# Attention over columns and a soft mixture of experts on one core: batches that share a tile of q and k, one set of 22 buffers, other split pairs and a new order

## The chip, the cores and the metric

The kernel runs on one core of a Trainium2 chip. The metric is the device time of one execution in microseconds, from the start of the program to its end. The engines are PE (TensorE, with its weight loads listed as PEld), DVE (VectorE), ACT (ScalarE), POOL (GpSimd) and SP (SyncE), which issues all DMA transfers of this kernel on one queue.

## The reference

Inputs are q, k and v of shape 4 x 5056 x 256, a scalar tau, phi (256 x 32) and the weights of eight experts, w1 (256 x 1024 each) and w2 (1024 x 256 each), all float32.

```python
qn = q / (norm(q, axis=1) + 1e-6)          # per batch and column, over the 5056 rows
kn = k / (norm(k, axis=1) + 1e-6)
a  = softmax(kn.T @ qn / tau)              # 256 x 256 per batch
x  = (v @ a).reshape(4 * 5056, 256)

logits = x @ phi                           # 20224 x 32
d  = softmax(logits, axis=0)               # over all rows
slot_input = d.T @ x                       # 32 slots, 4 per expert
slot_out[e] = relu(slot_input[e] @ w1[e]) @ w2[e]
out = softmax(logits, axis=1) @ slot_out   # 20224 x 256
```

## The kernel before

**Tiles.** A batch's 5056 rows are padded to 5120, ten units of four tiles of 128 rows; with four batches there are NU = 40 units, numbered u. `load_qk` (L127) brings q and k of one unit as 1 MB, 8 KB in each of 128 partitions, into a `raw` tile. v comes in twenty blocks p of eight tiles (`load_v`, L135, 1 MB). Each block's transpose `vt`, in two halves m of 512 KB (480 KB for a batch's last block), is needed for the logits: a half is either loaded (`load_vt`, L141 and L143, for the pairs in the set `LT`) or made on PE by four `turn` transposes (L355) per half block h, which ACT copies out of PSUM (`turned`, L360).

**Scores.** `score(u, j)` (L230) adds k.T @ q of one tile to a batch's sum in PSUM. In a raw tile it is one float32 matmul for each half of the columns. In a split tile, ACT casts q and k to a rounded high part (`cast`, L186), DVE subtracts to get the low part (`low`, L192), and three matmuls high x high, high x low, low x high take its place. The table `NS` splits the first two tiles of every unit but the first, 39 pairs. For the column norms ACT squares a unit (`square`, L207, tile `sq`) and DVE adds it to the batch's first `sq` tile (`add`, L213); `att_sums` folds that (L236).

**After a batch's scores** a chain of short `att_` steps makes the softmax `a` and M = a @ phi. `logits` (L383) multiplies the transposed v with M, and `gather` (L483) sums v under the row weights into slots. The last batch's slots go through the experts: `up` (L667), `flip_h`, `down` (L701) in two halves of the output columns, with w1 (`load_w1`, L651, eight loads of 1 MB) and w2 (`load_w2`, L656, sixteen loads of 512 KB, one per expert and half). `out_mul` (L741) and `out_evict` (L763 on ACT, L765 on DVE) make 1 MB output tiles, or halves of them for batch 0, and `store` (L771, L773) writes them.

**Buffers.** There are five `raw` tiles, three `sq`, three `hl` (high and low parts), six `v`, two `pre` tiles for early w2 loads, all 8 KB in a partition, and six `vt` tiles of 4 KB. `HOME` says which `raw` tile a unit takes; the others go round. A tile is used again once its last readers are done.

**Order.** Every step is put in a list by `at` or `tail`, and `ORDER`, a written permutation of that list, is the order in which they are issued. Each engine, and SP with its transfers, runs its own steps in that order. So a transfer whose buffer is not free yet holds back all transfers behind it.

Of the kernel before, what the change touches and what calls it, by code (L numbers as in the profile page):

```python
# [85 lines left out]
def colnorm_attention_soft_moe(  # L86
# [96 lines left out]
    def cast(u):  # L183
        ns = NS[u]
        hl = apool.tile([P, 2, 4, C], F32R, tag="hl", name=f"hl{u}", bufs=3)
        act.copy(hl[:, :ns, 0::2, :], raws[u][:, :ns])  # L186
        hls[u] = hl

    def low(u):
        ns = NS[u]  # L190
        hl = hls[u]
# [896 lines left out]
```

## Time and profile before

| What | Value |
|---|---|
| median of 3 runs | 280.6 us (280.35 to 280.88) |
| profiled execution | 279.4 us |
| its span, first to last instruction | 277.6 us |
| PE, DVE, ACT, POOL busy | 252.0, 233.1, 190.7, 7.4 us |
| moved by DMA | 112.98 MB, mean 407 GB/s |

The span is what the trace covers; the time of an execution has about 1.8 us more around it. The busy time of PE is made from matmuls whose ends are modelled, so short gaps between them do not show. A row of a timeline begins with the start and the length in us, and ends with the idle time of its engine before it and what ended that idle time.

### The profile page before, as it was taken

What the parts mean: (1) busy time and instruction counts of PE and PEld (TensorE: products, weight loads), DVE (VectorE), ACT (ScalarE), POOL (GpSimd) and SP (SyncE); (2) the same over time, 40 slices, a digit from 0 to 9 for tenths busy, and PEclk for the clock granted to TensorE, in tenths of its full rate; (3) what the DMA queues carried; (4) which work ended last, traced back from release to release, by engine and by line L of the source; (5) the groups of instructions that cost most, each with busy time, mean ns of one, the idle gap of its engine ahead of it and who ended that gap; (6) DMA issues with size and microseconds to landing.
All of it is one profiled execution on the core that took longest, in us unless ns stands there. A gap on an engine that the chain in (4) does not pass through costs nothing. (4 is left out here: it accounts for less than half of the span.)

```text
span 277.6 us, 6058 instructions
## 1 busy us (share of the span) xinstructions
PE 252.0 (91%) x2462; PEld 208.6 (75%) x2462; DVE 233.1 (84%) x343; ACT 190.7 (69%) x275; POOL 7.4 (3%) x10
## 2 busy tenths in 40 slices
PE   7998999999999999999999999999999999776600
PEld 7897999999898996999788878766544778466400
DVE  1598999999999999988998987559999879997620
ACT  4986898999898698897688943697417248544420
POOL 1000000200001100020000001000000000000000
PEclk9999999999999999999999999999999999955955
DMA  7999999999999999999999999999999999999996
GB/s 276 427 417 420 420 413 424 420 417 417 417 417 421 411 422 421 415 419 414 421 411 415 412 426 411 413 420 419 418 410 409 387 364 392 414 418 417 414 423 254
DMA packets 19179, 112.98 MB, mean 407 GB/s; under 512 B 2256, under 2 KB 2256, under 8 KB 8528
## 3 DMA queue, kind: packets, MB, share of 16 engines
q1 hardware_dynamic: 19152, 112.60, 98.9%
q8 instruction: 19, 0.31, 0.5%
q14 instruction: 8, 0.07, 0.1%
HBM read 91.62 MB, written 20.97 MB: 406 GB/s over the span
## 5 line engine op out<-in xcount | busy, mean ns | idle before, releaser
L213 DVE TENSOR_TENSOR sq<-sq,sq 128x1024 f32<-128x1024 f32 (+1 forms) x63 | 85.0, 1370 | 3.1 <-ACT sq L207 2.6
L207 ACT ACTIVATE sq<-raw 128x2048 f32<-128x2048 f32 x40 | 76.4, 1914 | 12.0 <-DMA raw<-in_qk_dram 5.9
L230 PE MATMUL S<-raw 128*128 128x256 f32 x328 | 76.8, 380 | 1.3 <-DMA raw<-in_qk_dram 1.3
L230 PE MATMUL S<-hl 128*128 128x256 f32 x468 | 68.3, 295 | 0.0
L230 PEld LDWEIGHTS S<-raw 128*128 128x128 f32 x328 | 59.8, 190 | 9.4 <-DMA raw<-in_qk_dram 2.2
L230 PEld LDWEIGHTS S<-hl 128*128 128x128 f32 x468 | 60.4, 190 | 1.3
L192 DVE TENSOR_TENSOR hl<-raw,hl 128x1024 fp32r<-128x1024 f32 x39 | 47.0, 1220 | 9.5 <-ACT hl L186 9.5
L186 ACT CAST hl<-raw 128x1024 fp32r<-128x1024 f32 x39 | 40.4, 1045 | 8.1 <-PE S L230 4.1
L741 PE MATMUL op_None<-so,lg 32*128 32x256 f32 x240 | 23.4, 481 | 6.0 <-DVE lg L631 4.1
L741 PEld LDWEIGHTS op_None<-so,lg 32*128 32x128 f32 x240 | 18.5, 231 | 10.3 <-ACT o L763 7.7
L763 ACT COPY o<-op_None 128x512 f32<-128x512 f32 x30 | 15.7, 594 | 15.2 <-PE op_None L741 7.8
L765 DVE COPY o<-op_None 128x512 f32<-128x512 f32 x30 | 19.0, 676 | 4.7 <-PE op_None L741 4.7
L355 PE MATMUL vTp<-ident,v 128*128 128x128 f32 x136 | 20.2, 277 | 0.0
L483 PE MATMUL G<-v,dn 128*32 128x256 f32 x320 | 19.5, 381 | 0.0
L355 PEld LDWEIGHTS vTp<-ident,v 128*128 128x128 f32 x136 | 15.7, 145 | 3.3 <-issue 1.2
L383 PE MATMUL L<-vt,M 128*32 128x256 f32 (+1 forms) x272 | 17.0, 379 | 0.0
L360 ACT COPY vt<-vTp 128x512 f32<-128x512 f32 x26 | 15.0, 582 | 2.6 <-PE vTp L355 2.6
L483 PEld LDWEIGHTS G<-v,dn 128*32 128x32 f32 x320 | 9.7, 110 | 7.1 <-issue 0.8
L383 PEld LDWEIGHTS L<-vt,M 128*32 128x32 f32 x272 | 8.5, 110 | 5.5 <-ACT x L360 0.3
L741 PE MATMUL op<-so,lg 32*128 32x128 f32 x160 | 8.9, 311 | 2.9 <-DVE o L765 1.7
L763 ACT COPY o<-op 128x256 f32<-128x256 f32 x20 | 6.4, 377 | 6.7 <-PE op L741 6.7
L252 POOL TENSOR_TENSOR rn<-rn,half 128x4 f32<-128x4 f32 x4 | 6.7, 1662 | 163.4 <-DVE rn L247 163.4
(111 smaller groups left out, 238.9 us busy)
## 6 DMA issues: line engine op xcount, KB each, us to landing
raw<-in_qk_dram SPq DMA_DIRECT2D x40, 1024.0 KB, 10.0
v<-in_v_dram SPq DMA_DIRECT2D x20, 1024.0 KB, 12.2
out_dram<-o SPq DMA_DIRECT2D x15, 1024.0 KB, 8.6
vt<-in_vt_dram SPq DMA_DIRECT2D x17, 512.0 KB, 11.0
w<-in_moe_w_dram SPq DMA_DIRECT2D x16, 512.0 KB, 11.0
w<-in_moe_w_dram SPq DMA_DIRECT2D x8, 1024.0 KB, 15.0
out_dram<-o SPq DMA_DIRECT2D x10, 512.0 KB, 4.7
vt<-in_vt_dram SPq DMA_DIRECT2D x4, 480.0 KB, 8.8
```

Source lines behind the costliest of these rows:

```text
L186: act.copy(hl[:, :ns, 0::2, :], raws[u][:, :ns])
L192: dve.tensor_tensor(hl[:, :ns, 1::2, :], raws[u][:, :ns], hl[:, :ns, 0::2, :].bitcast(F32), op=ALU.subtract)
L207: act.activation(sq, raws[u], AF.Square)
L213: dve.tensor_tensor(a[:, lo:hi], a[:, lo:hi], s[:, lo:hi], op=ALU.add)
L230: pe.matmul(sm, w, x, start=first, stop=False, skip_group_check=True)
L355: pe.transpose(tp[:, P * jj : P * jj + P], vs[p][:, 4 * h + jj, P * m : P * m + P], ident)
L360: act.copy(x[:, h * UT : h * UT + UT], tps[p, h, m])
L383: pe.matmul(L[S * g : S * g + S, :n, :], M[:, m, :], x[:, :n, S * g : S * g + S], start=m == 0, stop=m == 1,)
L483: pe.matmul(gp[S * g : S * g + S, :C], dn[:, x, j, :], vt[:, j, :], start=x == 0 and j < G, stop=x == n - 1 and j >= G,)
L741: pe.matmul(ops[b, p, hf, g][:, h, :], cT[b][S * g : S * g + S, 4 * i : 4 * i + 4, :].rearrange("s j t -> s (j t)"), so[S * g : S * g + S] ...
L763: act.copy(dst, src)
L765: dve.tensor_copy(dst, src)
```

## The change

- **Shared tiles.** Batches 0 and 1, and batches 2 and 3, are packed together: the last tile of unit 9 (and 29) holds the last 64 rows of one batch and the first 64 of the next (`MIX`). Unit 10 (and 30) then has three tiles. `score` does the mixed tile in two halves of 64 partitions, one for each batch's sum; `square_next` puts the second half's squares into the next batch's `sq` tile after a memset on POOL; `add` takes the rest in two pieces.
- **Split pairs.** `SPLIT` names 43 pairs of tiles (u, k), two tiles each, in place of `NS`. `cast` and `low` work on one pair, and each pair has a tile of its own.
- **Buffers.** All tiles of 8 KB are one set of 22, and `HOME` gives each its place: `raw`, `sq`, `hl`, `v`, the transposed v as `x` with both halves, `nat`, w1, w2, `hs`, `hT` and outputs.
- **w2** is laid out in blocks of 1 MB, two experts and one half of the columns each: eight loads.
- **vt.** (10, 0) and (14, 0) leave `LT` and are made by `turn` and `turned`, which now use two PSUM banks, T0 and X1, in place of T0 for most.
- The first load is issued as one tile and three tiles. `ORDER` is new.

The diff, with `HOME` and `ORDER` cut to the parts that are spoken of:

```diff
-NS = [0] + [2] * (NU - 1)
-LT = {(p, 0) for p in (0, 2, 3, 4, 5, 6, 7, 8, 9, 10, 11, 12, 13, 14, 15, 18, 19)} | {(p, 1) for p in (0, 3, 6, 9, 12, 15)}
+MIX = (UB - 1, 3 * UB - 1)
+SPLIT = {(u, 0) for u in range(1, NU) if u not in (1, 2, 3, 17, 20, 27, 31)} | {(u, 1) for u in (2, 5, 14, 24, 26, 27, 31, 33, 35, 37, 39)}
+LT = {(p, 0) for p in (0, 2, 3, 4, 5, 6, 7, 8, 9, 11, 12, 13, 15, 18, 19)} | {(p, 1) for p in (0, 3, 6, 9, 12, 15)}
...
+    "raw31": 11, "sq28": 9, "sq29": 6, "sq30": 14, "hl29_0": 18, "hl26_0": 5, "hl27_1": 16, "sq26": 10, "x7": 6,
+    "sq27": 21, "raw30": 15, "v3": 9, "v8": 21, "raw32": 3, "hl26_1": 15, "hl31_1": 18, "sq31": 1, "hl32_0": 20,
+    "sq32": 5, "hl30_0": 2, "x6": 10, "v11": 15, "raw33": 12, "raw34": 0, "raw37": 1, "raw38": 17, "hl33_1": 2,
+    "sq33": 15, "hl34_0": 10, "hl33_0": 8, "x8": 11, "sq37": 2, "sq34": 16, "hl37_1": 9, "raw39": 4, "v6": 12,
+    "v10": 7, "x9": 9, "x12": 1, "x11": 13, "raw36": 5, "raw35": 3, "hl38_0": 6, "sq39": 20, "hl37_0": 18, "sq38":
...
-    vpool = ctx.enter_context(tc.tile_pool(name="vpool", bufs=6, reuse_waits="tile"))
-    tpool = ctx.enter_context(tc.tile_pool(name="tpool", bufs=1, reuse_waits="tile"))
...
+    def big(name, shape, dt=F32):
+        return apool.tile(shape, dt, tag=f"big{HOME[name]}", name=name)
+
+    def tiles(u):
+        return 3 if u - 1 in MIX else 4
+
+    def load_qk(u, parts=None):
         b, i = divmod(u, UB)
-        raw = apool.tile([P, 4, 2, C], F32, name=f"raw{u}", **raw_home(f"raw{u}"))
-        for lo, hi in parts:
+        raw = big(f"raw{u}", [P, 4, 2, C])
+        for lo, hi in parts or ((0, tiles(u)),):
...
-    load_qk(0)
+    load_qk(0, ((0, 1), (1, 4)))
...
+    def cast(u, k):
+        hl = big(f"hl{u}_{k}", [P, 2, 4, C], F32R)
+        act.copy(hl[:, :, 0::2, :], raws[u][:, 2 * k : 2 * k + 2])
+        hls[u, k] = hl
...
     def square(u):
+        n = tiles(u)
+        act.activation(sq_tile(u)[:, :n], raws[u][:, :n], AF.Square)
+
+    def square_next(u):
+        sq = sq_tile(u + 1)
+        pool.memset(sq[:HD, 3], 0.0)
+        act.activation(sq[HD:, 3], raws[u][HD:, 3], AF.Square)
 
     def add(u, lo, hi):
         b, i = divmod(u, UB)
         a, s = sqs[b * UB], sqs[u]
-        dve.tensor_tensor(a[:, lo:hi], a[:, lo:hi], s[:, lo:hi], op=ALU.add)
+        if u in MIX and hi == 4:
+            if lo < 3:
+                dve.tensor_tensor(a[:, lo:3], a[:, lo:3], s[:, lo:3], op=ALU.add)
+            dve.tensor_tensor(a[:HD, 3], a[:HD, 3], s[:HD, 3], op=ALU.add)
+        else:
+            dve.tensor_tensor(a[:, lo:hi], a[:, lo:hi], s[:, lo:hi], op=ALU.add)
+
+    def score(u, j, split):
+        b = u // UB
+        mixed = u in MIX and j == 3
+        rows = ((b, 0, HD), (b + 1, HD, P)) if mixed else ((b, 0, P),)
...
-    def load_w2(e, h, tag):
-        if e not in w2t:
-            w2t[e] = slot(tag, f"w2_{e}").rearrange("p (x q) c -> p x (q c)", x=2)
-        sp.dma_start(w2t[e][:, h], w2[e, h][:, : NF * P])
+    def load_w2(k, h):
+        w2t[k, h] = big(f"w2_{k}_{h}", [P, 8, C]).rearrange("p (x q) c -> p x (q c)", x=2)
+        sp.dma_start(w2t[k, h], w2[k, h][:, : 2 * NF * P].rearrange("p (x f) -> p x f", x=2))
...
-                at(t, turn, p, h, m, T0)
+                at(t, turn, p, h, m, (T0, X1)[h])
...
-    x[:, :N, 0], x[:, :N, 1] = q, k
+    both = np.stack([q, k], axis=2)
+    x[0::2, :N] = both[0::2]
+    x[0::2, N:] = both[1::2, : P // 2]
+    n3 = 3 * P
+    x[1::2, :n3] = both[1::2, P // 2 : P // 2 + n3]
+    x[1::2, UT:] = both[1::2, P // 2 + n3 :]
```

## Rows read from the trace of the kernel before

**Rows 1.** The page: span, busy engines, GB/s by slice, the DMA queue, bytes.
```profile
span 277.6 us, 6058 instructions
...
PE 252.0 (91%) x2462; PEld 208.6 (75%) x2462; DVE 233.1 (84%) x343; ACT 190.7 (69%) x275; POOL 7.4 (3%) x10
...
GB/s 276 427 417 420 420 413 424 420 417 417 417 417 421 411 422 421 415 419 414 421 411 415 412 426 411 413 420 419 418 410 409 387 364 392 414 418 417 414 423 254
...
q1 hardware_dynamic: 19152, 112.60, 98.9%
...
HBM read 91.62 MB, written 20.97 MB: 406 GB/s over the span
```

**Rows 2.** Table by stage: stage, length, busy of PE/PEld/DVE/ACT/POOL, clock, DMA share, GB/s.
```profile
9.20:126.00 116.80, 115.91 (x832) 104.81 (x831) 111.77 (x115) 103.28 (x103) 5.64 (x3) 1.00 1.02 419
...
126.00:177.00 51.00, 51.00 (x503) 42.85 (x502) 43.68 (x76) 35.85 (x59) 1.01 (x1) 1.00 1.02 416
177.00:204.80 27.80, 27.13 (x362) 17.73 (x362) 22.94 (x65) 16.91 (x48) 0.00 (x0) 1.00 1.02 418
204.80:220.30 15.50, 15.09 (x228) 8.15 (x227) 14.94 (x18) 6.60 (x10) 0.00 (x0) 1.00 1.02 408
220.00:230.00 10.00, 9.53 (x249) 7.56 (x242) 8.11 (x18) 4.42 (x15) 0.00 (x0) 1.00 0.91 358
```

**Rows 3.** Waits of the SP queue: total us, times, longest us.
```profile
SPq L127 <- DVE hl L192: 58.8, 22, 4.4
```

**Rows 4.** Timeline of PE's weight loads that were held by a transfer.
```profile
165.80 0.59 PEld L483 LDWEIGHTS G<-v,dn 128*32 128x32 f32 x16 [0.36 <-DMA v<-in_v_dram]
...
205.73 0.16 PEld L667 LDWEIGHTS H<-w,slT 128*32 128x32 f32 x8 [0.83 <-DMA w<-in_moe_w_dram]
```

**Rows 5.** Timeline around the end of the reads: stores issued, the second half's `down`.
```profile
221.90 10.86 SPq L773 DMA_DIRECT2D out_dram<-o  x9
...
224.68 2.02 PE L701 MATMUL O<-w,hT 128*32 128x128 f32 x64
```

**Rows 6.** The page's DMA issues, w2: count, KB each, us to landing.
```profile
w<-in_moe_w_dram SPq DMA_DIRECT2D x16, 512.0 KB, 11.0
```

**Rows 7.** Timeline of the start: first loads issued, first and second landed.
```profile
0.74 2.56 SPq L127 DMA_DIRECT2D raw<-in_qk_dram  x5
...
5.61 1.91 ACT L207 ACTIVATE sq<-raw 128x2048 f32<-128x2048 f32 x1 [3.39 <-DMA raw<-in_qk_dram]
...
8.10 1.05 ACT L186 CAST hl<-raw 128x1024 fp32r<-128x1024 f32 x1 [0.57 <-DMA raw<-in_qk_dram]
```

**Rows 8.** PE: timeline of scores one behind another, and the group of transposes.
```profile
68.79 2.75 PE L230 MATMUL S<-raw 128*128 128x256 f32 x12
71.19 2.49 PE L230 MATMUL S<-hl 128*128 128x256 f32 x18
73.61 1.72 PE L383 MATMUL L<-vt,M 128*32 128x256 f32 x28
...
L355 PE MATMUL vTp<-ident,v 128*128 128x128 f32 x136 | 20.2, 277 | 0.0
```

**Rows 9.** Timeline of DVE: `low` and half adds one behind another.
```profile
65.51 1.22 DVE L192 TENSOR_TENSOR hl<-raw,hl 128x1024 fp32r<-128x1024 f32 x1
66.64 2.35 DVE L213 TENSOR_TENSOR sq<-sq,sq 128x1024 f32<-128x1024 f32 x2
68.91 1.22 DVE L192 TENSOR_TENSOR hl<-raw,hl 128x1024 fp32r<-128x1024 f32 x1
```

**Rows 10.** Groups by line and shape: count, busy us, mean ns, idle before.
```profile
L360 ACT COPY vt<-vTp 128x512 f32<-128x512 f32 x26 | 15.0, 582 | 2.6 <-PE vTp L355 2.6
...
L236 DVE TENSOR_TENSOR sq<-sq 128x512 f32<-128x512 f32 x4 | 2.7, 680 | 0.1
```

**Rows 11.** Timeline of the last `low` on DVE and the last scores on PE.
```profile
170.42 1.22 DVE L192 TENSOR_TENSOR hl<-raw,hl 128x1024 fp32r<-128x1024 f32 x1
...
175.32 1.68 PE L230 MATMUL S<-hl 128*128 128x256 f32 x12
```

More of the change, by code (lines that the diff above doesn't have):

```diff
@@ L133, in load_v @@
         b, i = divmod(p, PB)
-        vs[p] = slot("v" if p < 17 else "raw", f"v{p}")
+        vs[p] = big(f"v{p}", [P, 8, C])
         sp.dma_start(vs[p], v8[b, i][:, : 8 * C].rearrange("p (j c) -> p j c", c=C))
@@ L181, in colnorm_attention_soft_moe, with low, sq_tile @@
     hls = {}
[L183 to L191, printed above, removed]
+    def cast(u, k):
+        hl = big(f"hl{u}_{k}", [P, 2, 4, C], F32R)
+        act.copy(hl[:, :, 0::2, :], raws[u][:, 2 * k : 2 * k + 2])
+        hls[u, k] = hl
+    def low(u, k):
+        hl = hls[u, k]
         dve.tensor_tensor(
-            hl[:, :ns, 1::2, :], raws[u][:, :ns], hl[:, :ns, 0::2, :].bitcast(F32), op=ALU.subtract
+            hl[:, :, 1::2, :], raws[u][:, 2 * k : 2 * k + 2], hl[:, :, 0::2, :].bitcast(F32), op=ALU.subtract
         )
-    sqtag = {}
-    free = [0, 1, 2]
-    for b in range(B):
-        sqtag[b * UB] = free[0]
-        o = free[1:]
-        for i in range(1, UB):
-            sqtag[b * UB + i] = o[(i - 1) % 2]
-        free = [o[1], o[0], free[0]]
-    def square(u):
-        sq = apool.tile([P, 4, 2, C], F32, tag=f"sq{sqtag[u]}", name=f"sq{u}")
-        act.activation(sq, raws[u], AF.Square)
-        sqs[u] = sq
+    def sq_tile(u):
+        if u not in sqs:
+            sqs[u] = big(f"sq{u}", [P, 4, 2, C])
+        return sqs[u]
+    def square(u):
+        n = tiles(u)
[4 more added lines that the diff above has]
+        act.activation(sq[HD:, 3], raws[u][HD:, 3], AF.Square)
     def add(u, lo, hi):
@@ L212, in add @@
         a, s = sqs[b * UB], sqs[u]
-        dve.tensor_tensor(a[:, lo:hi], a[:, lo:hi], s[:, lo:hi], op=ALU.add)
-    def score(u, j):
-        b, i = divmod(u, UB)
-        first = "S" not in st[b]
-        if first:
-            st[b]["S"] = bank((S0, S1)[b % 2], f"S{b}")
+        if u in MIX and hi == 4:
[8 more added lines that the diff above has]
+        rows = ((b, 0, HD), (b + 1, HD, P)) if mixed else ((b, 0, P),)
+        first = {x[0]: "S" not in st[x[0]] for x in rows}
         for m in range(2):
-            sm = st[b]["S"][:, C * m : C * m + C]
             cols = slice(P * m, P * m + P)
-            if j >= NS[u]:
-                raw = raws[u]
-                ops_ = [(raw[:, j, 1, cols], raw[:, j, 0, :])]
-            else:
-                hl = hls[u]
-                ops_ = [(hl[:, j, x, cols], hl[:, j, y, :]) for x, y in ((2, 0), (2, 1), (3, 0))]
-            for w, x in ops_:
-                pe.matmul(sm, w, x, start=first, stop=False, skip_group_check=True)
-                first = False
+            for bb, lo, hi in rows:
+                if first[bb] and m == 0:
+                    st[bb]["S"] = bank((S0, S1)[bb % 2], f"S{bb}")
+                sm = st[bb]["S"][:, C * m : C * m + C]
+                if split:
+                    hl = hls[u, j // 2][:, j % 2]
+                    ops_ = [(hl[:, x, cols], hl[:, y, :]) for x, y in ((2, 0), (2, 1), (3, 0))]
+                else:
+                    raw = raws[u][lo:hi, j]
+                    ops_ = [(raw[:, 1, cols], raw[:, 0, :])]
+                for w, x in ops_:
+                    pe.matmul(sm, w, x, start=first[bb], stop=False, skip_group_check=True)
+                    first[bb] = False
     def att_sums(b, lo):
@@ L337, in att_m @@
         st[b]["M"] = M
-    tps, xs = {}, {}
+    tps = {}
+    xs = {}
     def vt_tile(p, m):
-        if (p, m) not in vts:
-            if p < 17:
-                vts[p, m] = tpool.tile([P, 8 * P], F32, tag=f"vt{m}", name=f"vt{p}_{m}", bufs=3)
-            else:
-                if p not in xs:
-                    xs[p] = apool.tile([P, 2, 8 * P], F32, tag=f"sq{XT[p]}", name=f"x{p}")
-                vts[p, m] = xs[p][:, m]
+        if p not in xs:
+            xs[p] = big(f"x{p}", [P, 2, 8 * P])
+        vts[p, m] = xs[p][:, m]
         return vts[p, m]
@@ L415, in logit_nat @@
         if b not in nat:
[L416 removed]
+            t = big(f"nat{b}", [P, 8, C]).rearrange("p j c -> p (j c)")
             nat[b] = t[:, : 8 * PB * S].rearrange("p (j s) -> p j s", s=S)
@@ L637, in colnorm_attention_soft_moe, with load_w1 @@
     w1t, w2t = {}, {}
-    def slot(tag, name):
-        if tag == "v":
-            return vpool.tile([P, 8, C], F32, tag="v", name=name)
-        if tag == "raw":
-            return apool.tile([P, 8, C], F32, name=name, **raw_home(name))
-        if tag == "hl":
-            return apool.tile([P, 8, C], F32, tag=tag, name=name, bufs=3)
-        return apool.tile([P, 8, C], F32, tag=tag, name=name, bufs=2 if tag == "pre" else None)
-    def load_w1(e, tag):
-        t = slot(tag, f"w1_{e}")
+    def load_w1(e):
+        t = big(f"w1_{e}", [P, 8, C])
         w1t[e] = t.rearrange("p (d x) c -> p d (x c)", d=2)
         sp.dma_start(w1t[e], w1[e][:, : 2 * F].rearrange("p (d f) -> p d f", d=2))
-    def load_w2(e, h, tag):
-        if e not in w2t:
-            w2t[e] = slot(tag, f"w2_{e}").rearrange("p (x q) c -> p x (q c)", x=2)
-        sp.dma_start(w2t[e][:, h], w2[e, h][:, : NF * P])
+    def load_w2(k, h):
+        w2t[k, h] = big(f"w2_{k}_{h}", [P, 8, C]).rearrange("p (x q) c -> p x (q c)", x=2)
+        sp.dma_start(w2t[k, h], w2[k, h][:, : 2 * NF * P].rearrange("p (x f) -> p x f", x=2))
     hss, hps, hTs, htp = {}, {}, {}, {}
@@ L662, in up @@
         if r not in hss:
-            hss[r] = tpool.tile([P, F], F32, tag="vt1", name=f"hs{r}", bufs=3)
+            hss[r] = big(f"hs{r}", [P, F])
         hp = bank(hb[r, x], f"H{r}_{x}")
@@ L687, in back_h @@
         if r not in hTs:
-            hTs[r] = tpool.tile([P, NF, P], F32, tag="vt0", name=f"hT{r}", bufs=3)
+            hTs[r] = big(f"hT{r}", [P, NF, P])
         (act.copy if x else dve.tensor_copy)(hTs[r][:, 4 * x : 4 * x + 4, :], htp[r, x])
@@ L703, in down @@
                     hTs[r][:, f, S * g : S * g + S],
-                    w2t[G * r + g][:, h, P * f : P * f + P],
+                    w2t[2 * r + g // 2, h][:, g % 2, P * f : P * f + P],
                     start=first and f == f0,
@@ L723, in o_back @@
         act.copy(sos[0][:, h], fo[h][:, :P])
-    OT = ["raw"] * 3 + ["hl"] * 3 + ["v"] * 6 + ["raw"] * 5 + ["hl"] * 3
     rings = {0: [S0, S1, LB, GB, T0, X0], 1: [S0, S1, LB, GB, T0, X0, T1, X1]}
@@ L752, in out_evict @@
         if (b, p) not in ots:
-            ots[b, p] = slot(OT[b * PB + p], f"o{b}_{p}")
+            ots[b, p] = big(f"o{b}_{p}", [P, 8, C])
         ot = ots[b, p]
@@ L791, in colnorm_attention_soft_moe @@
         first = i == 0
-        ns = NS[u]
-        if ns:
-            at(u - 1.08, cast, u)
-            at(u - (0.62 if first else 0.95), low, u)
+        for k in range(2):
+            if (u, k) in SPLIT:
+                at(u - 1.08, cast, u, k)
+                at(u - (0.62 if first else 0.95), low, u, k)
+                for j in (2 * k, 2 * k + 1):
+                    at(u + (0.45 if odd else 0.05) + 0.15 * j, score, u, j, 1)
         at(u - 0.65, square, u)
-        grp = [p for p in range(14) if 2 * p + FV == u and group(p)[2] == group(p)[3] - 1]
+        if u in MIX:
+            at(u - 0.64, square_next, u)
         if i:
@@ L803, in colnorm_attention_soft_moe @@
                 at(u + 0.60, add, u, 0, 4)
-        for j in range(ns):
-            at(u + (0.45 if odd else 0.05) + 0.15 * j, score, u, j)
         raw_at = u if first and u else u - (0.30 if u % 2 or u < FV else 0.04) if u else -0.6
-        for j in range(ns, 4):
-            at(raw_at + 0.001 * j, score, u, j)
+        for j in range(tiles(u)):
+            if (u, j // 2) not in SPLIT:
+                at(raw_at + 0.001 * j, score, u, j, 0)
         if u + NRAW < NU:
@@ L908, in colnorm_attention_soft_moe @@
                 t = 2.0 + 0.5 * (4 * (p - 15) + 2 * h + m)
-                tail(t, turn, p, h, m, (T0, T1)[h] if p > 15 else T0)
+                tail(t, turn, p, h, m, (T0, X1)[h])
                 tail(t + 0.05, turned, p, h, m)
@@ L977, in colnorm_attention_soft_moe @@
     tail(23.6, last_back)
-    for t, e, tag in (
-        (0.6, 0, "raw"), (0.6, 1, "raw"), (0.6, 2, "hl"), (0.61, 3, "hl"), (0.61, 4, "hl"),
-        (7.2, 5, "v"), (10.1, 6, "v"), (11.1, 7, "v"),
-    ):
-        tail(t, load_w1, e, tag)
-    for t, e, tag in (
-        (17.3, 0, "v"), (17.31, 1, "v"), (17.32, 2, "v"),
-        (19.2, 5, f"sq{XT[19]}"), (22.3, 6, "raw"), (22.4, 7, "raw"),
-    ):
+    for e in range(8):
+        tail(0.6 + e, load_w1, e)
+    for k in range(4):
         for h in range(2):
-            tail(t + 4 * h, load_w2, e, h, tag)
-    for e in (3, 4):
-        for h in range(2):
-            tail(20 + h, load_w2, e, h, "pre")
+            tail(17.3 + 4 * h, load_w2, k, h)
     for b, ts_ in ((0, (10.4, 10.5, 10.6, 13.8, 17.0, 17.1, 17.2)), (1, (18.9, 19.0, 19.1, 20.0, 20.5, 20.6, 20.7)),
@@ L1077 @@
     add("moe_w1", apart(w1.reshape(len(w1), P, -1)))
-    add("moe_w2", apart(w2.reshape(len(w2), P, -1, 2, P).transpose(0, 3, 1, 2, 4).reshape(len(w2), 2, P, -1)))
+    x = w2.reshape(len(w2) // 2, 2, P, -1, 2, P).transpose(0, 4, 2, 1, 3, 5)
+    add("moe_w2", apart(x.reshape(len(w2) // 2, 2, P, -1)))
     out_ap = nc.dram_tensor("out_0_dram", (B, PB, P, 2, 4 * C), F32, kind="ExternalOutput").ap()
```

5 lines of the change are left out of this document (removed), and 112 rows, old and new, of tables (HOME, ORDER).

## The prediction

> **What bounds the kernel now.** I read the page first, then the table by stage, then the waits, and then the timeline at the few places where they disagree. The page says that the one hardware DMA queue is busy 98.9% of the span, while GB/s stands near 417 in nearly every slice; PE is busy 91%, DVE 84%, ACT 69% [rows 1]. The table by stage makes it sharper: from 9.2 to 204.8 us the DMA share is 1.02 at 416 to 419 GB/s, PE is idle for 0.9 us in all up to 177 us, and DVE is busy 111.77 of 116.80 us up to 126 us [rows 2]. Three resources look full at once, so the question is which one the other two follow.
>
> Two things say DMA. The SP queue is held back mostly by DVE, which releases the q and k buffers (58.8 us in 22 waits) [rows 3], but the queue behind it never runs dry, or the rate would drop. And where PE's weight loads were held, some were held by transfers: at 165.80 us for a v block that had just landed, at 205.73 us, 0.83 us long, for w1 [rows 4]. Near the end of the reads, 2.0 us of `down` run at 224.68 us, nine stores are issued from 221.90 us on [rows 5], and the one dip of the rate lies there: 0.91 at 358 GB/s from 220 to 230 us, 0.9 us lost [rows 2]. After that the stores of 20.97 MB drain at the full rate. So the kernel is a read phase of 91.6 MB [rows 1], a short dip, and a write phase of 50 us (20.97 MB at 0.418 MB per us), with PE and DVE just keeping up.
>
> PE's busy share needs care: the rows have PE at 51.00 of 51.00 us from 126 to 177 us, but its weight loads (PEld) at 42.85, and at 17.73 of 27.80 us after that [rows 2]. The Trainium skill, Perfetto Trace Analysis (the note at its head), says that matmul busy time is a bad measure since matmuls are pipelined, and that the busy share of weight loads should be used. By PE's row there is no room and the second rival below is the forecast; by the rule, 16% of that stage is room. The waits for transfers agree with the rule.
>
> **The change part by part.**
>
> *Bytes.* Two units of q and k (u = 10 and 30) shrink from four tiles to three: 2 x 262,144 B = 0.52 MB. Two vt loads go, of 524,288 and 491,520 B: 1.02 MB. Together 1.54 MB; at the 417 GB/s of the stages they lie in [rows 2] that is **3.7 us**. It is worth that only while DMA sets the pace, so its other bound is 0. The Trainium skill, DMA: Bandwidth & Descriptors (Specifications), gives about 358 GB/s as the limit of HBM for one core. By it the same bytes would be an estimated 4.3 us. The rows show 417 held for 200 us, so the measurement decides.
>
> *w2 in 1 MB blocks.* The sixteen loads of 512 KB [rows 6] become eight of twice the size with the same 8.39 MB. The stage that holds most of them runs at 408 GB/s, its neighbour at 418 [rows 2]: 8.39 MB take 20.6 or 20.1 us. The slower rate may have another cause, so the bounds are 0 and 0.5; I take **0.3 us** saved. The eight issues less on SP are worth nothing, since SP waits for buffers.
>
> *First load in two parts.* The five first loads are issued from 0.74 us; the first lands at 5.61, the second at 8.10, 2.5 us per MB [rows 7]. The first quarter then lands about 1.9 us sooner, and PE starts one tile (0.8 us) earlier. That is room for PE, hidden behind DMA: nothing in the sum. DVE, however, starts later: its first operation is now the add of unit 1, behind a square that begins at 8.1 and takes 1.9 us [rows 7], so 10.0 instead of the 9.2 us at which a cast from 8.10 to 9.15 let it begin.
>
> *Split pairs.* 39 become 43. On PE a raw tile has 4 records, a split one 6; read from start to start, 12 raw records take 2.40 us (0.20 each) and 18 split ones 2.42 us (0.134) [rows 8]. Raw records go from 328 to 296 (ten tiles fewer, two of them counted twice because two batches share them), split ones from 468 to 516: -6.4 and +6.4 us, **0 on PE**. DVE does four more `low`, 1.13 us each from start to start [rows 9]: 4.5 us. ACT does four more casts of 1.05 us [rows 7], 4.2 us.
>
> *Two vt loads less.* Four more `turn` and `turned`: 16 transposes, by the group's mean of 0.149 us [rows 8] 2.4 us on PE (1.6 at the spacing 0.1 when dense), and four copies of 0.58 us on ACT [rows 10], 2.3 us. Turns now alternate between two PSUM banks instead of one, which can only loosen them.
>
> *Shared tiles.* Two squares shrink by a quarter (about -1.0 us on ACT), two half-tile squares and two POOL memsets are added, on 64 partitions by 512 elements; between nothing and the 0.68 us that DVE takes for a 128x512 add [rows 10] each. Two adds become two pieces, +0.2 us on DVE. ACT has 13 us of room up to 126 us and POOL is nearly empty [rows 2]; I take these at 0.
>
> *Buffers and order.* 5 + 3 + 3 + 6 + 2 tiles of 8 KB and 24 KB of vt tiles were 22 buffers, so the memory is the same. The first fourteen q/k units now need no release at all. What matters is where a later load takes a home that DVE releases. I went down the new order for each load's bytes ahead of it and the last reader of its home. The tightest are raw37 and raw36, in the homes of sq31 and sq32, free after DVE's adds of units 31 and 32. Ahead of raw37 are 58 DMAs with 52.4 MB; at 0.418 MB per us after the first landing at 5.6 its turn comes at 5.6 + 51.4 / 0.418 = 128.4 us. An empty queue needs 4.9 us from issue to landing, 2.5 of them transfer [rows 7], so raw37 must be issued by 126.0 us. DVE's work up to that add is 86 units of a half add or a `low`, the same number as before's DVE did in the 111.77 busy us up to 126 us [rows 2], and about 12 more small operations, some 2.4 us. Begun at 10.0 without any idle time it ends at 124.2; with the 5.0 us of idle time of that stretch of before [rows 2] at 129.2. So the queue loses between 0 and 3.2 us there; what is issued behind raw37 waits with it. Idle time was there in before for waits on ACT and PE that the new order has too, so I take the value nearer the upper end: **2.0 us** given back. The loads behind it, up to 158 us, have about 2 us of room; from the load of v16 on the homes come free 5 us and more ahead, but a queue that already runs at its full rate regains nothing.
>
> *The tail.* First output, stores and drain keep their shape; the 0.83 us wait for w1 goes, which is inside the 3.7. The dip at 220 us stays as it is: bounds 0 and -0.9, I take 0.
>
> Sum: -3.7 - 0.3 + 2.0 = **-2.0 us**. The profiled execution took 279.4 us (span 277.6), the median of the runs is 280.6, so 277.4 by the first and **278.6 us** by the second.
>
> **The rivals.**
>
> *Full gain.* DVE loses none of its time before unit 31: -4.0 us, 276.6, or 275.7 if the dip closes as well. For it: the split pairs are spread unevenly and can avoid the waits. Against: DVE had 5.0 us of idle time in just that stretch.
>
> *PE bounds, nothing changes.* PE's work grows by 1.6 to 2.4 us, less 0.8 for the early start and 0.8 for the w1 wait: 280.6 to 281.4. For it: 51.00 of 51.00 us. Against: PEld's row and the two waits for transfers [rows 2, 4].
>
> *Slower: DVE sets the end of the scores.* The last `low` of before starts at 170.42 and ends at 171.6; the last scores end at 177.0 [rows 11]. Its DVE work from 9.2 to there is 111.77 + 43.68 less about 2.7, 152.7 us, with 9.7 us idle. The new order adds 4.5 for `low`, 0.3 for split adds and about 1.8 for small operations set ahead: 159.3 from 10.0, so the last `low` ends at 169.3 plus the idle time x. Behind it come 24 score records and 8 transposes, 4.0 us: scores end at 173.3 + x against 177.0, and the tail has 8 transposes less, 0.8 us. It decides from x = 4.5 on. At x = 7.5 the time is +3.0 less the 0.8 of w1, 282.8; at before's 9.7, 285. Against: part of those 9.7 us came from waiting on transfers, which now come sooner.
>
> **How the numbers follow.** What a measurement of this kernel tells from no change is about 0.2%, 0.56 us. Partial gain, 277.4 to 280.0: 0.42. Full gain, 275.7 to 277.3: 0.25. No change: 0.13. Slower: 0.20, 281.2 to 285. Faster 0.67, same 0.13, slower 0.20. 276.0 to 282.0 leaves out about 0.04 below and 0.13 above; the likeliest case's own range is 277.4 to 280.0.
>
> **What would show it.** Right: 111.4 MB; a dip of the DMA share between about 125 and 145 us of 2 us in all, with SP waiting for sq and DVE's add; reads ending about 2 us sooner; DVE's busy share above 97% up to 126 us; w2's stage near 417. Full gain: no dip, the first store near 218 us. PE bound: dips spread out, first store near 222. Slower: PE waiting for DVE's `low` after 130 us, the last scores past 178. Most wrong would be my count of small operations on DVE, or an order in which waits of ACT on PE, which I have not priced, come into play.

## The result, and the profile of the changed kernel

The changed kernel took 277.12 us (median of 4, 276.88 to 278.42), the kernel before 280.74 us beside it: the ratio is 0.9879, with a 95% interval of 0.9844 to 0.9914, so 3.4 us less (2.4 to 4.4). Run again beside the first experiments it took 278.26 us, ratio 0.9922 (0.9893 to 0.9952). Its eight times fall into two groups, four from 276.88 to 277.25 and four from 278.23 to 278.61; their median is 277.7. The profiled execution took 277.06 us, 2.3 us less than that of before. The forecast was 278.6 us, in a range of 276.0 to 282.0.

The page of the changed kernel: span, busy engines, GB/s in 40 slices, the DMA queue, bytes.
```profile
span 275.3 us, 6127 instructions
...
PE 254.6 (92%) x2494; PEld 212.6 (77%) x2494; DVE 236.8 (86%) x349; ACT 195.5 (71%) x285; POOL 7.5 (3%) x12
...
GB/s 283 432 424 410 422 426 415 420 417 419 419 417 420 412 422 421 416 415 417 412 419 418 416 417 419 417 416 420 421 415 420 300 332 388 418 418 412 420 421 246
...
q1 hardware_dynamic: 17856, 111.06, 98.0%
...
HBM read 90.08 MB, written 20.97 MB: 403 GB/s over the span
```
The bytes are those of the forecast, 1.54 MB less. A slice is 6.9 us long. The lowest slice of before has 364 GB/s and begins at 222 us [rows 1]; here the dip is deeper (300, 332), and its lowest slice begins at 213 us. The table by stage says where (columns as in [rows 2]):
```profile
9.20:126.00 116.80, 116.80 (x885) 104.91 (x887) 114.41 (x125) 105.43 (x109) 5.77 (x5) 1.00 1.01 418
126.00:177.00 51.00, 51.00 (x502) 45.41 (x495) 47.60 (x74) 40.82 (x68) 1.01 (x1) 1.00 1.02 418
177.00:204.80 27.80, 27.51 (x365) 17.21 (x367) 23.08 (x67) 15.23 (x48) 0.00 (x0) 1.00 1.01 417
204.80:216.00 11.20, 11.02 (x204) 6.94 (x199) 11.06 (x13) 5.90 (x8) 0.00 (x0) 1.00 1.02 422
216.00:218.00 2.00, 1.87 (x40) 1.10 (x29) 1.71 (x3) 0.27 (x1) 0.00 (x0) 1.00 0.75 303
218.00:220.00 2.00, 2.00 (x51) 1.56 (x55) 1.28 (x3) 0.70 (x3) 0.00 (x0) 1.00 0.42 172
220.00:230.00 10.00, 9.24 (x219) 8.04 (x218) 7.91 (x21) 5.52 (x18) 0.00 (x0) 1.00 0.83 332
126.00:145.00 19.00, 19.00 (x205) 16.57 (x198) 18.83 (x26) 18.20 (x25) 0.00 (x0) 1.00 1.02 420
```
Up to 216 us the transfers run at their full rate and lose nothing; the stretch where the forecast put a dip, 126 to 145 us, has a share of 1.02 at 420 GB/s. Counted in full rate, the queue's work ends at about 217.5 us (three quarters of the two us from 216); in the kernel before it ends near 221.7 (0.85 of the two us from 220, the first row below). So the reads gained 4.2 us. The last load says the same: the last block of w2 is issued at 200.37 us and lands 19.9 us later, at 220.2; in the kernel before it is issued at 214.57, takes 10.1 us and lands at 224.7, so the reads gained 4.5 us by this count. The stage of before, and the time from issue to landing of that last load, changed kernel and before:
```profile
220.00:222.00 2.00, 2.00 (x62) 1.48 (x51) 1.84 (x3) 0.65 (x2) 0.00 (x0) 1.00 0.85 336
...
DMA to landing us min/median/max: 19.9/19.9/19.9
...
DMA to landing us min/median/max: 10.1/10.1/10.1
```
Before, the first store was issued at 221.90 us [rows 5], 2.8 us ahead of that last landing, so stores filled the queue while the reads ran out. Now it comes only 0.7 us ahead of it: from 217 us on the last two blocks of w2 land with nothing queued behind them, and the share falls to 0.42 (218 to 220 us). Timeline of SP: the load of `raw37`, that of `raw36`, the first store.
```profile
123.69 0.33 SPq L146 DMA_DIRECT2D raw<-in_qk_dram  x1
...
130.94 0.33 SPq L146 DMA_DIRECT2D raw<-in_qk_dram  x1
...
219.54 10.89 SPq L782 DMA_DIRECT2D out_dram<-o  x9
```
The first store is 2.36 us sooner than before, and the end 2.3; from the first store to the end of the span it is 55.7 us in both. What sets the first store lies mostly on the engines, as the experiments show. Timelines of DVE (its first operation, the add of unit 31, the last `low`) and of PE (last scores, the logits behind them, the first `up`, the first `out_mul`), and of PE in the kernel before (`up`, the first `out_mul`):
```profile
10.01 2.29 DVE L235 TENSOR_TENSOR sq<-sq,sq 128x2048 f32<-128x2048 f32 x1 [7.83 <-ACT sq L220]
...
121.31 2.32 DVE L235 TENSOR_TENSOR sq<-sq,sq 128x1024 f32<-128x1024 f32 x2
...
169.29 1.22 DVE L209 TENSOR_TENSOR hl<-raw,hl 128x1024 fp32r<-128x1024 f32 x1
```
```profile
173.90 2.40 PE L255 MATMUL S<-hl 128*128 128x256 f32 x18
...
177.61 1.07 PE L403 MATMUL L<-x,M 128*32 128x256 f32 x16
...
202.67 5.36 PE L677 MATMUL H<-w,slT 128*32 128x512 f32 x48
...
217.36 1.34 PE L750 MATMUL op<-so,lg 32*128 32x128 f32 x16
```
```profile
204.75 6.32 PE L667 MATMUL H<-w,slT 128*32 128x512 f32 x48
...
220.30 0.73 PE L741 MATMUL op<-so,lg 32*128 32x128 f32 x16
```
The add that frees the home of `raw37` ends at 123.6 us, and the load follows at once. From 10.01 us DVE is idle for 1.6 us up to 126 us (114.41 busy of 115.99) where before it lost 5.0. The last `low` ends at 170.5 us (171.6 before), the scores at 176.3 (177.0), `up` starts at 202.67 (204.75) and takes 5.36 us (6.32, of it 0.83 the wait for w1 [rows 4]), and the first `out_mul` starts at 217.36 (220.30).

### The profile page after: what moved, and what is told of

It reads as the page before. It is cut to its first block, busy times and chain, and to the rows that moved or that the text cites. A ratio compares the mean times of both kernels' runs of the same rounds, so it can differ in the third digit from the quotient of the medians.

```text
span 275.3 us, 6127 instructions
## 1 busy us (share of the span) xinstructions
PE 254.6 (92%) x2494; PEld 212.6 (77%) x2494; DVE 236.8 (86%) x349; ACT 195.5 (71%) x285; POOL 7.5 (3%) x12
## 4 chain that ended last, share of the span: by engine, by line
PE 87%; DVE 6%; ACT 3%; issue 1%; DVEq 0%; ACTq 0%
PE S L255 46%; PE op_None L750 8%; PE L L403 7%; PE G L503 7%; PE vTp L376 6%; PE op L750 3%; PE O L711 2%; DVE o L774 2%; ACT o L772 2%; PE wake L787 2%; PE Mp L347 1%; PE nn L266 1%; DVE nat L630 1%; DVE cm L627 1%; PE sp L549 1%; PE gt L525 1%
## 5 line engine op out<-in xcount | busy, mean ns | idle before, releaser
L235 DVE TENSOR_TENSOR sq<-sq,sq 128x1024 f32<-128x1024 f32 (+1 forms) x61 | 81.3, 1356 | 8.4 <-ACT sq L220 8.0
L220 ACT ACTIVATE sq<-raw 128x2048 f32<-128x2048 f32 (+1 forms) x40 | 74.7, 1889 | 6.5 <-DMA raw<-in_qk_dram 4.8
L255 PE MATMUL S<-raw 128*128 128x256 f32 (+1 forms) x296 | 66.9, 384 | 0.0
L255 PEld LDWEIGHTS S<-hl 128*128 128x128 f32 x516 | 65.2, 191 | 1.0
L255 PEld LDWEIGHTS S<-raw 128*128 128x128 f32 (+1 forms) x296 | 53.7, 192 | 8.1 <-issue 1.5
L209 DVE TENSOR_TENSOR hl<-raw,hl 128x1024 fp32r<-128x1024 f32 x43 | 51.6, 1219 | 0.7 <-ACT hl L204 0.7
L381 ACT COPY x<-vTp 128x512 f32<-128x512 f32 x38 | 21.5, 593 | 9.3 <-PE vTp L376 8.8
L403 PE MATMUL L<-x,M 128*32 128x256 f32 (+1 forms) x320 | 20.3, 379 | 0.0
L403 PEld LDWEIGHTS L<-x,M 128*32 128x32 f32 x320 | 9.8, 109 | 6.2 <-issue 0.8
L750 PEld LDWEIGHTS op<-so,lg 32*128 32x128 f32 x160 | 7.7, 197 | 4.4 <-ACT o L772 2.7
```

The costliest lines, as they stand in the source:

```text
L209: dve.tensor_tensor(hl[:, :, 1::2, :], raws[u][:, 2 * k : 2 * k + 2], hl[:, :, 0::2, :].bitcast(F32), op=ALU.subtract)
L220: act.activation(sq_tile(u)[:, :n], raws[u][:, :n], AF.Square)
L235: dve.tensor_tensor(a[:, lo:hi], a[:, lo:hi], s[:, lo:hi], op=ALU.add)
L255: pe.matmul(sm, w, x, start=first[bb], stop=False, skip_group_check=True)
L381: act.copy(x[:, h * UT : h * UT + UT], tps[p, h, m])
L403: pe.matmul(L[S * g : S * g + S, :n, :], M[:, m, :], x[:, :n, S * g : S * g + S], start=m == 0, stop=m == 1,)
```

## The experiments

All are edits of the changed kernel, timed beside the kernel before; where two are compared, the difference of their ratios is taken times 280.5 us. The control is the changed kernel itself; "the first run" is that of the section on the result. Each ratio is known to 0.4 to 1.0 us, so a difference of under 1 us is no finding by itself.

> The changed kernel as it is, run again beside the others: both theories 277.1 us, 3.5 us under the kernel before, the first store issued near 219.5 us and the reads at their end near 217.4 us. Theory A (the engines' work up to the first output sets the end; transfers have 2 to 3 us to spare behind the reads). Theory B (transfers still set the end; every MB is worth 2.4 us).

278.26 us. Its profile has the same pace up to `up` (202.51 us), but the granted clock fell there (columns as in [rows 2]):
```profile
202.00:203.00 1.00, 1.00 (x9) 0.66 (x12) 0.93 (x3) 0.18 (x1) 0.00 (x0) 0.79 1.00 418
203.00:206.00 3.00, 3.00 (x20) 0.74 (x16) 3.00 (x3) 0.00 (x0) 0.00 (x0) 0.50 1.02 415
206.00:207.00 1.00, 1.00 (x16) 0.34 (x12) 1.00 (x2) 0.69 (x1) 0.00 (x0) 1.00 1.02 426
```
At 0.50, the lower of the two levels (1.2 GHz), `up` took 7.05 us in place of 5.36, the first `out_mul` came at 218.64 and the first store at 220.74 us, 1.2 later. That is about the distance between the two groups of times, and three of the control's four times are in the upper group; e10 takes it up. Of the first run's four, three are in the lower group, so a time between the two says little.

**e1, more bytes.**
```diff
+        if p in (8, 18):
+            sp.dma_start(xs[p], vt8[b, i].rearrange("m p w -> p m w")[:, :, : 8 * P])
```


> Two loads of transposed v are doubled in size: 1.05 MB more is read, 2.5 us at 417 GB/s, and no engine does anything else. Theory A: the reads end 2.5 us later, near 219.9 us, just when the first store is ready; the first store stays at 219.5 and the time grows by 0 to 0.7 us. Theory B: 2.5 us slower than the control, first store near 222.

279.69 us, ratio 0.9968 (0.9943 to 0.9994): 1.3 us over the control, between the theories. The median lies between two groups of times, four from 278.63 to 279.11 and six from 280.28 to 280.56 us, and the profile is of the upper one. PE's weight loads show a wait that neither had:
```profile
181.12 0.59 PEld L405 LDWEIGHTS L<-x,M 128*32 128x32 f32 x16 [2.13 <-DMA x<-in_vt_dram]
```
These are the logits behind the last scores, waiting for block 13's half of transposed v, a load queued behind both of those that were doubled. So one transfer in the middle had next to no room, whatever there was behind w2. (In this execution ACT could take up the rest of the first unit only at 7.24 instead of 5.65 us, and all that follows is 1.6 us later. `up` took 5.36 us, so the clock did not fall there.)

**e2, fewer bytes at the end.**
```diff
     def load_w2(k, h):
+        if k == 3:
+            return
...
-                    w2t[2 * r + g // 2, h][:, g % 2, P * f : P * f + P],
+                    w2t[min(2 * r + g // 2, 2), h][:, g % 2, P * f : P * f + P],
```


> The last two blocks of w2 (experts 3 and 7 of the layout's last pair, both halves) are not loaded and the block before stands in for them, so the output is not the reference's: 2.10 MB less is read, 5.0 us at 417 GB/s, at the end of the reads, and no engine does less. Theory A: the reads end near 212.4 us, the first store stays at 219.5 +/- 0.3 us and the time within 0.5 us of the control. Theory B: 4 to 5 us faster.

276.41 us, ratio 0.9864 (0.9839 to 0.9889): 1.6 us under the control, 0.4 under the first run. The queue is nearly empty from 214 us on:
```profile
214.00:216.00 2.00, 2.00 (x80) 1.83 (x68) 1.97 (x4) 0.00 (x0) 0.00 (x0) 1.00 0.14 57
216.00:218.00 2.00, 2.00 (x49) 1.47 (x49) 1.56 (x3) 0.44 (x2) 0.00 (x0) 1.00 0.05 12
```
Yet the first `out_mul` starts at 217.09 us (217.36 in the changed kernel) and the first store at 218.69 (219.54).
```profile
217.09 0.73 PE L752 MATMUL op<-so,lg 32*128 32x128 f32 x16
```
```profile
218.69 10.86 SPq L784 DMA_DIRECT2D out_dram<-o  x9
```
Five us of transfer bought 0.9 us between the profiles (span 274.4 against 275.3), where theory B asks for 4 to 5: it falls for the end of the reads. (0.6 us of that one is the length of the first `out_mul`, 0.73 for 1.34; the profile names no cause.)

**e3, less PE.**
```diff
-                    ops_ = [(hl[:, x, cols], hl[:, y, :]) for x, y in ((2, 0), (2, 1), (3, 0))]
+                    ops_ = [(hl[:, x, cols], hl[:, y, :]) for x, y in ((2, 0), (2, 1), (3, 0))[: 2 if u >= 30 else 3]]
```


> In the 14 split pairs of the last batch the third product (low x high) is left out, so the output is not the reference's to full precision: 56 records of 0.134 us, 7.5 us, less on PE alone. Theory A with PE as the engine that sets the pace: the last scores and the first expert matmul come 4 to 7 us sooner, until the reads (end at 217.4 us) hold the stores: 2 to 2.5 us faster than the control. Theory A with DVE or ACT as the pace: the first expert matmul moves by under 1.5 us and the time by under 1 us. Theory B: no change.

276.89 us, ratio 0.9886 (0.9859 to 0.9914): 1.0 us under the control, 0.2 over the first run: no gain that can be told. The scores end at 174.6 us, 1.7 sooner for 7.5 us less work, and `up` starts at 202.08, 0.6 sooner. What PE meets in between (weight loads and what held them):
```profile
175.71 0.42 PEld L376 LDWEIGHTS vTp<-ident,v 128*128 128x128 f32 x4 [0.90 <-ACT x L381]
...
177.03 0.59 PEld L403 LDWEIGHTS L<-x,M 128*32 128x32 f32 x16 [0.63 <-DMA x<-in_vt_dram]
```
So PE is not alone in setting the pace, and PE now waits for block 13's half, which lands at 177.0 us; in the changed kernel it lands at 176.7, 0.9 ahead of its use (177.61). The first store comes at 218.68 us, as in e2, but the span ends at 275.1, 0.7 later than there: the last block of w2 still lands at 220.4.
```profile
218.68 11.78 SPq L782 DMA_DIRECT2D out_dram<-o  x9
```
So once the first store comes that early, the end of the reads seems to count again: it had about 1 us to spare, not the 2 to 3 of theory A.

**e4, more DVE.**
```diff
     def low(u, k):
         hl = hls[u, k]
-        dve.tensor_tensor(
+        for _ in range(2 if (u, k) in ((28, 0), (29, 0)) else 1):
+            dve.tensor_tensor(
```


> Two `low` of units 28 and 29 are done twice over, with the same result: 2 x 1.13 = 2.3 us more on DVE between 90 and 115 us, nothing else. Theory C (DVE without idle time sets the pace of the scores, and everything behind moves with it): the add of unit 31 ends at 126 instead of 123.6 us, the last scores and the first expert matmul are 1.5 to 2.3 us later, the time 1.5 to 2.3 us longer. Theory P (the prediction's step: the add that frees the home of raw37 must end by 126.0 us, transfers set the end): the DMA share dips by 0 to 0.5 us behind 126 us, the time grows by no more than that. Theory E (PE sets the pace): under 0.5 us.

279.16 us (12 times, 278.91 to 279.69), ratio 0.9966 (0.9952 to 0.998): 1.2 us over the control, 2.4 over the first run, 2.3 between the profiles. PE waits for the `low`, and everything behind is 2.0 us later: scores to 178.3, `up` at 204.67, first `out_mul` at 219.36 us.
```profile
115.29 0.89 PEld L256 LDWEIGHTS S<-hl 128*128 128x128 f32 x7 [1.66 <-DVE hl L210]
```
The load of `raw37` is issued at 125.91 us, just inside the prediction's limit of 126.0. GB/s from 126 to 145 us is lower than the 420 of the changed kernel:
```profile
126.00:145.00 19.00, 19.00 (x212) 16.26 (x208) 18.79 (x28) 18.25 (x24) 0.00 (x0) 1.00 1.00 401
```
But hardly a load behind it lands later. `raw37` itself takes 6.0 us from its issue and lands at 131.9 us; in the changed kernel it takes 7.9 and lands at 131.6 (131.7 in the control). The loads that land from 137 to 178 us do so within 0.2 us of those of the changed kernel. The times to landing of `raw37`, changed kernel and e4:
```profile
DMA to landing us min/median/max: 7.9/7.9/7.9
...
DMA to landing us min/median/max: 6.0/6.0/6.0
```
So the loss that the prediction feared is not seen here, and the 2 us came by way of the engines alone: theory C.

**e5 and e7, fewer `low`.** e5 takes four pairs out of the split set; e7 also moves a load.
```diff
-SPLIT = ... | {(u, 1) for u in (2, 5, 14, 24, 26, 27, 31, 33, 35, 37, 39)}
+SPLIT = ... | {(u, 1) for u in (2, 5, 14, 24, 26, 27, 31)}
```


> Four pairs of the last batch (units 33, 35, 37 and 39, second pair) are raw again: 4 `low` of 1.13 us and 4 casts of 1.05 us less, 4.5 us on DVE and 4.2 us on ACT; PE does 32 records of 0.20 us in place of 48 of 0.134, the same 6.4 us. Theory C: the scores end 2 to 4 us sooner, then the half block of transposed v for block 13, which lands near 177.0 us, holds PE: the first expert matmul 0.5 to 1 us sooner, the time 0.3 to 1 us shorter. Theory E (PE): no change.

> As the run with four pairs raw again, and the load of transposed v for block 13 is set ahead of that for block 18, so that it lands 1.25 us sooner. If that landing is what holds PE behind the scores, the first expert matmul comes 1.2 to 2.2 us sooner than in the changed kernel and the time is 1 to 2 us shorter, until the reads (end at 217.4 us) hold the first store. If it is not, the same as with four pairs raw alone.

279.70 us, ratio 1.0002 (0.9979 to 1.0026), and 279.95 us, 0.9994 (0.9978 to 1.0011): 2 us slower than the control (e5's profile is of its lower group of times, 279.34 to 279.81; five of twelve lie from 280.95 to 281.63), against the expectation. A raw tile that is not split is read by PE itself, so its home is free only when PE has come that far, and the queue waits. SP's longest wait from 143 to 165 us, and the stage from 152 to 156 us (both of e5):
```profile
SPq L158 <- PE S L253: 9.3, 1, 9.3
```
```profile
152.00:156.00 4.00, 4.00 (x29) 3.79 (x28) 3.96 (x7) 3.41 (x11) 0.00 (x0) 1.00 0.32 119
```
4 us at a share of 0.32 are 2.7 us lost, and from there on every load lands 2.8 us later than in the changed kernel. Setting block 13's load first lets `up` start 1.0 us sooner (203.56 against 204.60), but `down` then waits 1.3 us for w2, which is as late as in e5. The two runs say nothing on DVE; they price a home that is released late.

**e6, the two vt loads back.**
```diff
-LT = {(p, 0) for p in (0, 2, 3, 4, 5, 6, 7, 8, 9, 11, 12, 13, 15, 18, 19)} | ...
+LT = {(p, 0) for p in (0, 2, 3, 4, 5, 6, 7, 8, 9, 10, 11, 12, 13, 14, 15, 18, 19)} | ...
```


> The two half blocks of transposed v, (10, 0) and (14, 0), are loaded again in place of 16 transposes and 4 copies: 1.05 MB more to read, 2.5 us, of it all ahead of the half block for 13; 1.6 to 2.4 us less on PE, 2.3 us less on ACT, nothing less on DVE. If transfers have room the time is the same or up to 1 us shorter. If the landing of block 13's half, 0.6 us ahead of its use, is the second limit: it lands near 179.5 us, the first expert matmul comes 1.5 to 2 us later, and the time is 1.5 to 2 us longer; so the two loads dropped are worth that much.

280.40 us (278.81 to 281.62), ratio 1.0008 (0.9984 to 1.0033): 2.4 us over the control. The profiled execution, 281.54 us, is one of the slowest. Block 13's half lands at 179.3 us, as worked out; PE stands for 2.9 us, and then runs at the lower clock:
```profile
179.29 0.20 PEld L402 LDWEIGHTS L<-x,M 128*32 128x32 f32 x8 [3.31 <-DMA x<-in_vt_dram]
```
```profile
179.00:185.00 6.00, 5.71 (x56) 2.77 (x60) 0.42 (x1) 0.48 (x2) 0.00 (x0) 0.50 1.02 422
```
`up` starts at 207.26 us, 4.6 later. 1.7 of it is the landing against its use in the changed kernel (179.29 against 177.61). Nearly all of the other 2.9 is the clock: the same three groups of logits and `gather` behind the wait take 1.93, 3.64 and 1.45 us where the changed kernel has 1.07, 1.91 and 1.03. The two fastest times of e6, 278.81 us, are 1.7 over the changed kernel's lower group, which is what the landing alone would cost; no profile of them exists.

**e8, less DVE without touching a home.**
```diff
     def add(u, lo, hi):
...
+        if u in (26, 28):
+            return
```


> The adds of units 26 and 28 are left out (four halves of 1.13 us, 4.5 us of DVE near 100 to 112 us), so two units are missing from one batch's norms; their squares are still made and no release comes later. Theory C (DVE first, PE and the landing of block 13's transposed v less than 1 us behind it): the scores end 0.5 to 1.7 us sooner, PE then waits for block 13 near 177 us, the first expert matmul comes 0.3 to 0.8 us sooner, the time 0.3 to 1 us shorter than the changed kernel (whose eight times so far have a median of 277.7). If DVE alone held the kernel: 2 us and more. If DVE does not hold it: no change.

277.34 us (276.74 to 279.10), ratio 0.9892 (0.986 to 0.9924): no gain that can be told. The profiled execution is the slowest of the six: from 32 us on its loads land some 0.6 us later than the changed kernel's, the scores end at 177.0 us, and the clock fell in `up`, which took 6.91 us. DVE now stands where it did not before, for ACT's squares and for PE:
```profile
103.31 1.23 DVE L237 TENSOR_TENSOR sq<-sq,sq 128x1024 f32<-128x1024 f32 x1 [0.80 <-ACT sq L220]
108.86 1.23 DVE L237 TENSOR_TENSOR sq<-sq,sq 128x1024 f32<-128x1024 f32 x1 [1.13 <-ACT sq L220]
...
118.36 0.16 DVE L273 COPY rn<-nn 128x4 f32<-128x4 f32 x1 [1.59 <-PE nn L268]
```
So 2.3 us more on DVE cost 2 us, and 4.5 us less bring no gain that can be told. The waits, with those of e3, suggest that DVE, ACT, PE and the landing of block 13's half reach the end of the scores within about 1 us of each other.

**e9, the two small parts undone.**
```diff
-    load_qk(0, ((0, 1), (1, 4)))
+    load_qk(0)
...
+        for x in range(2):
+            sp.dma_start(w2t[k, h][:, x], src[:, x])
```


> The first load in one piece again and w2 in sixteen pieces of 512 KB again. By the prediction's terms: 0.3 us more in the reads for w2, nothing for the first load. Theory C: PE's start 0.6 to 0.8 us later is hidden, since DVE's first add still starts at 10.0; the reads end up to 0.3 us later, behind which there are 2 us of room: the time within 0.3 us of the changed kernel.

278.01 us (277.43 to 278.63), ratio 0.9902 (0.9875 to 0.9928), the same as the changed kernel. The stage of w2 does run slower with the smaller blocks, at 410 GB/s against 422, and the last block lands 0.6 us later (220.8 us), which the time does not show:
```profile
204.80:216.00 11.20, 11.02 (x196) 6.86 (x192) 11.06 (x13) 6.04 (x8) 0.00 (x0) 1.00 1.03 410
```

**e10, three idle matmuls** (two records of 0.23 us each). One each behind `last_z`, `last_acc` and `last_slots`, into bank T1.
```diff
-    def wake(k, tb=X0):
+    def wake(k, tb=X0, n=0):
...
+    for n in range(3):
+        at(99, wake, 1, T1, n)
```


> Three idle matmuls into an unused bank, 0.23 us each, are put into PE's waits between the last gather and the first expert matmul (200 to 202.7 us). In one of two profiles of the changed kernel the granted clock there fell to 0.50 for 3 us and the first output came 1.3 us later. If the short waits bring that about: the runs near 278.4 go away and the median is 277.1, at the price of up to 0.2 us. If not: the same two groups of times, median 277.7.

276.89 us (276.83, 276.86, 276.89, 277.58, 277.72), ratio 0.9878 (0.9849 to 0.9907). `up` starts 0.3 us later, at 202.95, and runs through at the full clock:
```profile
202.55 0.47 PE L786 MATMUL wake<-ones 128*128 128x128 f32 x2
202.95 5.36 PE L676 MATMUL H<-w,slT 128*32 128x512 f32 x48
```
```profile
203.00:206.00 3.00, 3.00 (x33) 0.91 (x36) 3.00 (x3) 0.69 (x1) 0.00 (x0) 1.00 1.00 412
```

**e11, a version with small gains together.** e10; `back_h(0, 1)` ahead of `c_exp(2)`; squares and adds of units 1 and 2 in halves, and unit 1 loaded in two parts.
```diff
+        for lo, hi in ((0, 2), (2, 4)) if u in (1, 2) else ((0, n),):
+            act.activation(sq_tile(u)[:, lo:hi], raws[u][:, lo:hi], AF.Square)
```


> A version that might be faster than both: the three idle matmuls; the copy of the first hidden half (0, 1) on ACT ahead of one exponential of the output softmax, which lets the last relu start 0.3 us sooner; the squares and adds of units 1 and 2 in halves and the load of unit 1 in two parts, so that DVE starts near 8.5 instead of 10.0 us. Theory C: DVE's start is worth 0.3 to 0.8 us at the end of the scores, together 0.3 to 1.2 us faster than the changed kernel. If PE or the transfers hold the scores: only the 0.3 us of the copy.

277.05 us (276.85 to 277.52), ratio 0.9873 (0.9845 to 0.9901): below the median of the changed kernel in either run, but by less than the noise, and not faster than e10. DVE starts at 8.35 instead of 10.01 us and waits the lead off again:
```profile
8.35 2.36 DVE L236 TENSOR_TENSOR sq<-sq,sq 128x1024 f32<-128x1024 f32 x2 [6.18 <-ACT sq L220]
11.51 1.23 DVE L208 TENSOR_TENSOR hl<-raw,hl 128x1024 fp32r<-128x1024 f32 x1 [0.80 <-ACT hl L203]
...
35.63 1.23 DVE L208 TENSOR_TENSOR hl<-raw,hl 128x1024 fp32r<-128x1024 f32 x1 [0.93 <-ACT hl L203]
```
The scores end at 176.28 us, where they ended. None of the nine times of e10 and e11 is above 277.72, four of eight of the changed kernel are above 278.2. But e2 and e3 have no time above 277.79 in eight either, without these matmuls.

## Why the prediction came out, and which of its steps did not

**The size was right by two errors.** -2.0 us was forecast, -2.3 measured between the profiles, -3.4 and -2.2 between the medians. The mechanism of the partial gain was the wrong one, and that the time came out near the forecast is luck: the loss that was put at +2.0 us was 0, and a loss at the end of the reads that was put at 0 was about as large. The time alone could not tell: the first median, 277.12, lies in the range of the rival "full gain" (275.7 to 277.3), the second, 278.26, in that of the likeliest case. The prediction's own signs could: of those for a partial gain the bytes and DVE's share (114.41 of 116.80 us, 98%) came, the dip before 145 us did not, and the reads ended 4 us sooner in place of 2.

**Bytes and w2** (-3.7 and -0.3): right as work of the queue. Its work ends 4.2 us sooner by the rate, 4.5 by the last landing, and e9 shows the block size at 410 against 422 GB/s. By the 358 GB/s of the Trainium skill, DMA: Bandwidth & Descriptors (Specifications), the bytes would be worth an estimated 4.3 us; the runs go on at 417 to 422, so the trace's price stood.

**+2.0 us given back at `raw37` and `raw36`**: the step that failed. I kept the 5.0 us of DVE's idle time of before [rows 2] and put the add at 129.2 us at the worst; the idle time was 1.6 us and the add ended at 123.6, even ahead of my best case of 124.2. 3.4 of the 5.6 us between 129.2 and 123.6 are waits that the new order does not have, the rest is my count of DVE's work, 114.2 us where the trace has 112.1 from 10.01 to 123.63 us. (A slip beside it changes nothing: 51.4 / 0.418 is 123.0, so the limit would be 126.2.) The limit itself was not put to the test: in e4 the load is issued at 125.9 us, still inside it, and the loads behind it land as before. That a late home costs queue time is shown elsewhere, by e5. Which edit removed the waits (other pairs, order, two PSUM banks) was not taken apart.

**What gave the time back instead**: the tail, which the prediction put at 0 ("the dip at 220 us stays as it is", bounds 0 and -0.9). The sum ended at the reads and took for granted that the first output follows them, since before the two fell together. The first store came only 2.4 us sooner, and the queue lost 3.4 us from 216 to 230 us (shares of 0.75, 0.42 and 0.83) where it lost 0.9 before. That the transfers did not hold the first store is shown by e2 (5 us of transfer less at the end, 0.9 us gained). That the engines' chain sets it, with block 13's half close beside it, is shown from one side by e4 and e6; the edits that relieved one of them brought no gain beyond the noise (e3, e8).

**PE, 0 for the splits**: consistent; raw records are 296, split ones 516, and PE's rows are full as before. The second rival read that as the bound. The Trainium skill, Perfetto Trace Analysis (the note at its head), which has matmul busy time as a bad measure, is borne out: PE's row stayed at 51.00 of 51.00 us between 126 and 177 us while that of weight loads went from 42.85 [rows 2] to 45.41, and 7.5 us less PE work moved the scores' end by 1.7.

**DVE sets the end (the slower rival)**: its own condition decided. Its end of the last `low`, 169.3 + x, decides from 173.8 us on and came out at 170.5. (DVE's work up to there was 157.1 us, not 159.3, and its idle time 3.4.) The rival was right on the path, though: DVE's work does reach the end, and e4 shows how near it was: each us more on DVE there is nearly a us on the end.

**Full gain**: nearly right on the transfers (no dip), wrong on the tail: the first store is at 219.5, not 218 us.

**Vt loads**: the 1.02 MB count, but by another way than in the sum. Put back (e6), they cost 2.4 us by the medians, near their 2.5 us of queue, but through block 13's half, which lands only 0.9 us ahead of its use, and through the clock behind that wait, and not through the end of the reads.

Open: the 0.6 us in the first `out_mul`, and what sets the two groups of times.

## What to carry to other kernels

Bytes saved are worth their rate only up to the point where the next resource is: before summing, take the first thing behind the transfers (here the first store) and ask how much sooner the engines could have it ready with the transfers gone. Where several resources are full at once, an edit that loads one of them can cost nearly its full price (2.3 us on DVE cost 2) and one that relieves it bring almost nothing (4.5 us less brought no gain that can be told). A wait of an engine in the old trace belongs to the old order; keep it as a bound, not as a term. A lower rate in a stretch is not yet a loss: look whether the loads behind it land later (in e4 they did not). And with homes written by hand, count who reads a tile last: moving a read from DVE to PE kept the queue waiting 9.3 us.
